# Turning the rows of the first layer's second block: VectorE squares read back from DRAM, with the scaling on Pool, against sixteen transposes on TensorE

## The chip, the cores and the metric

The kernel runs on one core of one Trainium2 chip. The metric is the device time of one execution in microseconds. Before the change it is 1894.93 us, the median of three runs (1894.68 to 1895.23).

## What is computed

Two layers, each of them an attention block and a gated block, over 2048 rows of 448 features. Both layers use the same weights.

```
x = x + A(layernorm(x), wqkv, wo)
x = x + B(layernorm(x), w_gate, w_up, w_down)
(and both once more)

A(x): q, k, v = x @ wqkv                      # 16 heads of 28
      softmax(q k^T * 28**-0.5) v, @ wo
B(x): (sigmoid(x @ w_gate) * (x @ w_up)) @ w_down
```

layernorm subtracts the mean of a row and divides by sqrt(variance + 1e-5); it has no weights. All inputs and the output are float32.

## The kernel before, in words

The 2048 rows are 16 row tiles of 128 (`NT`), and four of them (`TB`) make a block of 512 rows (`W`), so there are four blocks, b0 to b3. Matrix products are made in float16 with both operands split into a high and a low part: a product of two split operands is three matmuls, high by high, low by high and high by low.

The instructions go to each engine in the order in which the program emits them; there is no scheduler. Each engine works through its own list in order, and waits where it reads what another engine or a transfer has yet to write. SP (SyncE) and Pool (GpSimd) also issue DMAs from their lists, in order too: a DMA that has to wait keeps the ones behind it waiting.

Each layer begins with `project` (from L712 on): for each block the queries and keys and then the values are made from the block's normalized rows.

- `qk` (L725) makes queries and keys of one block in seven tiles. A tile is 11 matmuls of 128x512 (L564), accumulated in one of four banks of PSUM in turn. ScalarE evicts the high part (L756), VectorE the low part (L757), both look at squares (L759, L761) that TensorE sums later (L735, L738), and SP stores the tile to a scratch tensor in DRAM (L764). After tile i the function calls `fill[i]`, work of other kinds that is put there by hand.
- `vals` (L784) makes the values of one block, a row tile at a time: 11 matmuls of 128x448 (L586 to L591), in the same four banks, evicted by ScalarE (L793). Between the products of row tile j and its eviction it calls `after[j]`, again work put there by hand. For block 0 that list is `along_values`.

For these products a block has to be normalized and turned, so that features lie along the partitions. The kernel has two ways for it, both in class `Block`:

- Over TensorE: VectorE computes mean and variance of a row tile (L287, L288), Pool the reciprocal root of the variance (L291, L293), VectorE scales (`scale`, L320), TensorE turns 128x128 pieces into PSUM (`turn`, L508), ScalarE casts the high part from PSUM (`turned_high`, L532) and VectorE subtracts to get the low part (`turned_low`, L540 and L543). A block has 16 such transposes, four row tiles by four groups of features.
- Over DRAM: after the same norm and scaling VectorE turns each row tile in squares of 32 by 32 (`squares`, L337), SP stores the squares to DRAM in four DMAs (`store`, L349), reads them back in two with the squares put in their places (`gather`, L357 and L359), and ScalarE and VectorE split the result from SBUF (`part`, reached through `ready`: L218, L219, L223, L224). The read back waits for all four stores, and stands behind them in SP's list.

In the first layer b0 and b1 go the first way and b2 and b3 the second. In the second layer all but b0 go the second way.

The order around the change, for the first layer and block 0: the norms of b1's row tiles 0 and 1 come after tile 2 of `qk`, those of 2 and 3 after tile 3, the scaling of all four on VectorE after tile 5 (`fill` at L836). Between the value products of b0 come, after row tile 0, the allocation of b1's operands, eight transposes of b1 with their splits, and two loads for measuring the sizes of the weights (`tell.read`, L935 on, issued by SP); after row tile 1 the other eight transposes and two loads; after row tile 2 the maxima of the norms of b0 (`fin`, L775), b2's norms and a load issued by Pool; after row tile 3 b2's squares and store and another group of loads by Pool (`along_values` at L838 to L841). Then `qk` of b1 begins on TensorE.

At the very start, before any data have come, TensorE runs products of zeros (`keep_busy`, L261).

Of the kernel before, what the change touches and what calls it, by code (L numbers as in the profile page):

```python
# [19 lines left out]
P = 128  # L20
# [7 lines left out]
TB = NT // NB  # L28
W = TB * P
NF = F // P  # L30
NQ = D // 32
# [87 lines left out]
def interleaved_layers(ctx: ExitStack, tc: tile.TileContext, x_in, wqkv, wo, w_gate, w_up,  # L119
                       w_down, out):  # L120
    nc = tc.nc
# [6 lines left out]
    big = Slots(spool, "s", N_SLOTS)  # L128
# [26 lines left out]
    x = cpool.tile([P, NT, D], F32, name="x")  # L155
# [107 lines left out]
    class Block:  # L263
# [52 lines left out]
            nc.vector.transpose(self.xs[:, :, j, :], v)  # L316
            qrt.put(v)

        def scale(self, j):
            nc.vector.tensor_scalar(self.xn[:, j, :], x[:, self.b * TB + j, :],  # L320
                                    self.mv[:, j, 0:1], self.rs[:, j:j + 1],
                                    op0=ALU.subtract, op1=ALU.mult)

# [56 lines left out]
        def squared(self):  # L380
            return [lambda j=j: self.norm_two(j) for j in range(0, TB, 2)] + [
                lambda j=j: self.lift(j) for j in range(TB)] + [
                    lambda j=j: self.square(j) for j in range(TB)]
# [328 lines left out]
    def project(layer, wq, begun):  # L712
# [4 lines left out]
        def ones_of_values():  # L717
            for v in values:
                nc.gpsimd.memset(v[:, :, :, DH:VC], 0.0)
                nc.gpsimd.memset(v[:, :, :, DH:DH + 1], 1.0)  # L720
# [99 lines left out]
        idle = None  # L820
        sq = lambda b, *js: lambda: blks[b].squares(js)
        b1, b2, b3 = blks[1:]
        if layer == 0:
            def scaled():
                b1.xn = big.get("xn", [P, TB, D])
                for j in range(TB):
                    b1.scale(j)

            def turned(kts):
                b1.turn_banks(6, kts)  # L830
                for j in range(TB):
                    b1.turn(j)
                b1.turned_high()
                b1.turned_low()

            fill = [idle, idle, lambda: b1.norm([0, 1]), lambda: b1.norm([2, 3]), idle, scaled]  # L836
            tell = Measure()
            along_values = {0: lambda: (b1.parts(), turned([0, 1]), tell.read(2)),  # L838
                            1: lambda: (turned([2, 3]), big.put(b1.xn), tell.read(2)),
                            2: lambda: (fin(), b2.norm(), tell.read()),  # L840
                            3: lambda: (b2.squares(), b2.store(), tell.read())}  # L841
        else:
            ones_of_values()
            fill = [idle, lambda: b1.ready(0, 1), lambda: b1.ready(2, 3), b2.norm,
                    lambda: b2.squares([0, 1]), sq(2, 2, 3), b2.store]
            along_values = {0: b3.norm, 1: sq(3, 0, 1), 2: lambda: (fin(), b2.gather()),
                            3: sq(3, 2, 3)}
        fin = qk(0, blks[0], fill, None)
        vals(0, blks[0], along_values)
        if layer == 0:  # L850
            fill = [b2.gather, b3.norm, sq(3, 0, 1), sq(3, 2, 3), idle,
                    lambda: b2.ready(0, 1), lambda: (b2.ready(2, 3), b3.store())]
        else:
            fill = [idle, lambda: b2.ready(0, 1), lambda: b2.ready(2, 3), b3.store]
        fin = qk(1, b1, fill, None)
        vals(1, b1, {0: b3.gather, 2 if layer == 0 else 1: fin})
        add = tell.add if layer == 0 else idle
        fin = qk(2, b2, [idle, lambda: b3.ready(0, 1), lambda: b3.ready(2, 3), idle, add, add,
                         add], None)
        fin = qk(3, blks[3], [add, add, add], fin)  # L860
# [1005 lines left out]
    for layer in range(LAYERS):  # L1866
        values, heads, last_values = project(layer, wq, begun)
        gate = WeightsGated()
        outs = attend(layer, values, heads, last_values, gate, wq.keep)
        mlp_first = out_project(outs, gate)  # L1870
        wq = WeightsQKV()

        def before_next(f, wq=wq):
            if f == NF - 1:
                wq.load()

        begun = gated(layer, mlp_first, gate, before_next)
# [28 lines left out]
```

## Time and profile before

| | |
|---|---|
| median of three runs | 1894.93 us |
| span of the profiled execution, first to last instruction | 1893.0 us |
| what the median lies above the span | 1.93 us |
| busy TensorE / VectorE / ScalarE / Pool, share of the span | 100% / 76% / 73% / 12% |
| granted TensorE clock, mean | 1.000 |
| mean DMA rate | 143 GB/s |

How to read the rows that follow. A row of the order of time has the start and the duration in us, the engine, the line, the operation, what it writes and reads, the count of instructions that were merged into it, and in brackets the idle time of the engine before it with what ended it. PE is TensorE, DVE is VectorE, ACT is ScalarE, SPq is SP's list of DMA issues (the duration there is the issue, not the transfer). Matmuls are pipelined, so the duration of one is longer than the distance between two. A row of the waits has who waited for whom, and then the total in us, the number of times and the longest. A row of a group by tile has the smallest, median and largest duration in ns behind the count. A row by line has the busy time in us and the mean in ns behind the bar. A row of a table of stretches has the busy time of PE, PEld, DVE, ACT and POOL (each with its count of instructions), the granted clock, the mean share of time that the DMA engines were busy, and GB/s.

### The profile page before, as it was taken

The numbers are of one execution on the slowest core, as the hardware profiler recorded it, in microseconds if no ns is written. First come the engines' busy times: TensorE is split into PE (matmuls) and PEld (weight loads), VectorE is DVE, ScalarE is ACT, GpSimd is POOL, SyncE is SP. The second block draws the span as 40 slices with busy tenths as digits, with TensorE's granted clock in tenths as the row PEclk, the third lists the DMA queues.
The fourth block names the chain that finished last, engine by engine and source line by source line (L and its number), as shares of the span: only waits on it lengthen the run. The fifth ranks groups of instructions, "written<-read, shape, count | busy, mean of one in ns | idle before, by whom it ended". The sixth has DMA issues, their size and how long they took to land. (4 is left out here: it accounts for less than half of the span.)

```text
span 1893.0 us, 56282 instructions
## 1 busy us (share of the span) xinstructions
PE 1886.5 (100%) x24254; PEld 1323.1 (70%) x24254; DVE 1430.7 (76%) x2835; ACT 1382.7 (73%) x1772; POOL 231.5 (12%) x453
## 2 busy tenths in 40 slices
PE   9999999999999999999999999999999999999999
PEld 4455555555556799999954556667666567999998
DVE  7758989898976688787564487787778676887664
ACT  5569999999993566555345799999999745565541
POOL 3023112222101111111100000000000020121110
PEclk9999999999999999999999999999999999999999
DMA  7676454334323566646734322122120245666553
GB/s 247 194 212 166 132 137 128 107 119 129 103 88 121 192 205 235 231 181 238 251 96 134 90 52 47 32 52 52 31 48 24 67 160 174 218 251 223 208 208 142
DMA packets 110882, 270.86 MB, mean 143 GB/s; under 512 B 13214, under 2 KB 67838, under 8 KB 110496
## 3 DMA queue, kind: packets, MB, share of 16 engines
q0 software_dynamic: 31776, 158.51, 23.4%
q1 hardware_dynamic: 78288, 108.20, 20.3%
q8 instruction: 192, 3.15, 0.7%
q10 hardware_dynamic: 560, 0.46, 0.1%
q14 instruction: 66, 0.54, 0.1%
HBM read 207.88 MB, written 50.85 MB: 137 GB/s over the span
## 5 line engine op out<-in xcount | busy, mean ns | idle before, releaser
L1222 ACT ACTIVATE prob_s<-sc 128x1536 f32<-128x1536 f32 (+1 forms) x657 | 887.9, 1487 | 6.6 <-PE sc L1207 5.9
L1258 PE MATMUL acc<-prob_s,val_s 128*32 128x256 f32 (+3 forms) x7700 | 569.9, 383 | 0.0
L1207 PE MATMUL sc<-qp_s 114*32 114x512 f16 x7868 | 553.2, 379 | 0.0
L579 PEld LDWEIGHTS <-gu_s 128*128 128x128 f16 x4368 | 426.9, 98 | 46.8 <-issue 0.4
L1207 PEld LDWEIGHTS <-qp_s 114*32 114x32 f16 x8192 | 272.7, 95 | 203.4 <-issue 88.3
L1258 PEld LDWEIGHTS acc<-prob_s,val_s 128*32 128x32 f32 x7700 | 272.3, 110 | 142.9 <-issue 13.6
L579 PE MATMUL chain<-xwide_s,gu_s 128*128 128x256 f16 x2016 | 247.5, 273 | 0.0
L1552 PE MATMUL dnp<-dn_s,hparts_s 128*128 128x224 f16 x2016 | 225.2, 259 | 0.0
L1552 PEld LDWEIGHTS <-hparts_s 128*128 128x128 f16 x2016 | 194.0, 98 | 4.4
L1238 DVE SCALAR_TENSOR_TENSOR power_q<-power_q,expo_q 128x512 f32<-128x512 f32 x243 | 168.2, 692 | 8.3
L1625 ACT COPY one_q<-chain 128x256 f32<-128x256 f32 x224 | 82.4, 371 | 121.4 <-PE chain L579 120.8
L1641 DVE TENSOR_TENSOR one_q<-side,one_q 128x512 f32<-128x512 f32 x112 | 72.2, 686 | 101.8 <-PE side L579 101.5
L579 PE MATMUL side<-xshort_s,gu_s 128*128 128x256 f16 x1120 | 140.5, 273 | 0.0
L564 PE MATMUL qkp<-xhl_s,wqk_s 128*128 128x512 f16 x616 | 138.1, 379 | 0.7 <-ACT wqk_s L231 0.2
L564 PEld LDWEIGHTS <-wqk_s 128*128 128x128 f16 x616 | 60.1, 98 | 69.8 <-ACT wqk_s L231 1.1
L1437 POOL DMA_DIRECT2D gu_s<-gu_parts x104 | 56.0, 538 | 430.5 <-PE side L579 424.5
L1287 DVE STREAM_TRANSPOSE oturned_q<-acc 128x512 f32<-128x512 f32 x32 | 22.9, 716 | 97.1 <-PE acc L1258 96.9
L1258 PE MATMUL acc<-power_q,val_s 128*32 128x256 f32 (+3 forms) x300 | 94.2, 396 | 0.0
L579 PE MATMUL side<-xwide_s,gu_s 128*128 128x256 f16 x672 | 91.6, 273 | 0.0
L1505 ACT CAST hparts_s<-hsums_q 128x256 f16<-128x256 f32 (+1 forms) x136 | 65.0, 494 | 30.2 <-DVE hsums_q L1517 20.2
L756 ACT ACTIVATE qkhl_q<-qkp 128x512 f16<-128x512 f32 x56 | 33.2, 593 | 71.9 <-PE qkp L564 68.3
L1652 ACT ACTIVATE one_q<-one_q 128x512 f32<-128x512 f32 x56 | 35.2, 629 | 64.3 <-DVE one_q L1641 64.3
(218 smaller groups left out, 2318.0 us busy)
## 6 DMA issues: line engine op xcount, KB each, us to landing
gu_s<-gu_parts POOLq DMA_DIRECT2D x104, 800.0 KB, 6.0
dn_s<-dn_parts POOLq DMA_DIRECT2D x42, 784.0 KB, 7.8
qp_s<-qk_scr SPq DMA_DIRECT2D x96, 224.0 KB
qk_scr<-qkhl_q SPq DMA_DIRECT2D x56, 256.0 KB
gu_parts<-pack_s POOLq DMA_DIRECT2D x14, 800.0 KB, 3.8
xt_scr<-xs_s SPq DMA_DIRECT2D x48, 224.0 KB
xraw_s<-xt_scr SPq DMA_DIRECT2D x12, 768.0 KB
qp_s<-qk_scr SPq DMA_DIRECT2D x64, 112.0 KB
```

Source lines behind the costliest of these rows:

```text
L564: nc.tensor.matmul(pm, w, x, start=(i == 0), stop=(i == len(terms) - 1))
L579: nc.tensor.matmul(pm, a, x, start=(first and i == 0), stop=(i == len(terms) - 1), skip_group_check=True)
L1207: nc.tensor.matmul(ps[32 * j:32 * j + 32, :], hd.k[:, keys], hd.q[:, qb * W:(qb + 1) * W], start=True, stop=True, tile_position=(0, 32 * j))
L1222: nc.scalar.activation(prob[:, 0:n, :], ps[:, 0:n, :], AF.Exp, scale=exp_scale)
L1238: nc.vector.scalar_tensor_tensor(p, p, c[k], y, op0=ALU.add, op1=ALU.mult)
L1258: nc.tensor.matmul(acc[qb * VC:(qb + 1) * VC, s], v[:, kc % TB, h, :], probs[c * NB + qb][:, s], start=(kc == 0 and a == 0), stop=(kc == N ...
L1437: queue.dma_start(self.gu[-1][m], gu_parts[p, m])
L1505: nc.scalar.copy(to[:, :, 0], a)
L1552: nc.tensor.matmul(pm, a[:, x, t], w[:, p, y], start=(begin and n == 0 and (j == 0 or alone)), stop=(n == 2), skip_group_check=True)
L1625: nc.scalar.copy(to, pm)
L1641: nc.vector.tensor_tensor(one[m], side[m], one[m], op=ALU.add)
L1652: nc.scalar.activation(out, v, AF.Sigmoid, scale=gate_scale)
```

## The change

Block b1 of the first layer goes the second way instead of the first. Its scaling moves from VectorE to Pool. The norms move one `qk` tile forward (after tiles 1 and 2), the scaling follows after tile 3, the squares after tiles 4 and 5, and store and read back after tile 5, ahead of the store of tile 6 in SP's list. The splits come between the value products of b0, after row tiles 2 and 3. What stood there moves: b2's norms come after row tile 0, two of its squares after row tile 1, the other two with `fin` and b2's store after row tile 3. The second layer is as before.

```
-        def scale(self, j):
-            nc.vector.tensor_scalar(self.xn[:, j, :], x[:, self.b * TB + j, :],
+        def scale(self, j, engine=nc.vector):
+            engine.tensor_scalar(self.xn[:, j, :], x[:, self.b * TB + j, :],
                                     self.mv[:, j, 0:1], self.rs[:, j:j + 1],
                                     op0=ALU.subtract, op1=ALU.mult)
...
             def scaled():
                 b1.xn = big.get("xn", [P, TB, D])
+                b1.xs = big.get("xs", [P, NQ, TB, 32])
                 for j in range(TB):
-                    b1.scale(j)
-
-            def turned(kts):
-                b1.turn_banks(6, kts)
-                for j in range(TB):
-                    b1.turn(j)
-                b1.turned_high()
-                b1.turned_low()
-
-            fill = [idle, idle, lambda: b1.norm([0, 1]), lambda: b1.norm([2, 3]), idle, scaled]
+                    b1.scale(j, nc.gpsimd)
+
+            def squared(*js):
+                for j in js:
+                    nc.vector.transpose(b1.xs[:, :, j, :], b1.xn[:, j, :])
+                if js[-1] == TB - 1:
+                    big.put(b1.xn)
+                    b1.store()
+                    b1.gather()
+
+            fill = [idle, lambda: b1.norm([0, 1]), lambda: b1.norm([2, 3]), scaled,
+                    lambda: squared(0, 1), lambda: squared(2, 3)]
             tell = Measure()
-            along_values = {0: lambda: (b1.parts(), turned([0, 1]), tell.read(2)),
-                            1: lambda: (turned([2, 3]), big.put(b1.xn), tell.read(2)),
-                            2: lambda: (fin(), b2.norm(), tell.read()),
-                            3: lambda: (b2.squares(), b2.store(), tell.read())}
+            along_values = {0: lambda: (b2.norm(), tell.read(2)),
+                            1: lambda: (sq(2, 0, 1)(), tell.read(2)),
+                            2: lambda: (b1.ready(0, 1), tell.read()),
+                            3: lambda: (b1.ready(2, 3), fin(), sq(2, 2, 3)(), b2.store(),
+                                        tell.read())}
```

## The prediction

> **What bounds the kernel now.** I read the page first, then the list of waits of TensorE, then the order of time around the change.
>
> ```profile
> span 1893.0 us, 56282 instructions
> ...
> PE 1886.5 (100%) x24254; PEld 1323.1 (70%) x24254; DVE 1430.7 (76%) x2835; ACT 1382.7 (73%) x1772; POOL 231.5 (12%) x453
> ...
> PE 44%; DVE 0%; issue 0%
> ```
>
> ```profile
> PE still L261 <- DVE warm L179: 1.3, 1, 1.3
> PE turn L508 <- DVE xn_s L320: 0.8, 1, 0.8
> PE qkp L564 <- ACT wqk_s L231: 0.2, 1, 0.2
> PE qkp L564 <- DVE xhl_s L543: 0.2, 1, 0.2
> ```
>
> The second fence is the whole list for the whole span: TensorE waits four times, 2.5 us in all. So TensorE sets the end, and every microsecond taken from its queue or put into it moves the end by as much, since nothing behind it has idle time to give. The question is what its queue looks like between 30 and 50 us, where the first layer goes from block 0 to block 1:
>
> ```profile
> 33.48 1.66 PE L508 MATMUL turn<-ident,xn_s 128*128 128x128 f32 x8
> 34.98 0.35 PE L589 MATMUL vp<-wv_s,xhl_s 128*128 128x448 f16 x1
> ...
> 37.07 1.04 PE L508 MATMUL turn<-ident,xn_s 128*128 128x128 f32 x8
> 37.94 0.35 PE L589 MATMUL vp<-wv_s,xhl_s 128*128 128x448 f16 x1
> ...
> 42.43 9.66 PE L564 MATMUL qkp<-xhl_s,wqk_s 128*128 128x512 f16 x44
> 51.92 0.27 PE L735 MATMUL qnorm<-sq_q,ind 128*128 128x256 bf16 x1
> ```
>
> The two groups of eight transposes stand between value products of block 0; at 42.43 block 1's products begin, 44 of them in 9.49 us, so 0.216 each and 2.37 for a tile of 11.
>
> **What it removes.** The first group holds the queue from 33.48 to 34.98 (part of it waiting for the last scaled rows), the second from 37.07 to 37.94: 1.50 + 0.87 = 2.37 us. Without them TensorE asks for block 1's operands at 42.43 - 2.37 = 40.06. The four evictions of the transposes on ScalarE and VectorE give way to four casts and four subtractions from SBUF of the same kind, and cost nothing new.
>
> **What it adds: a chain that has to end at 40.06.** It is norms, Pool's scaling, VectorE's squares, store, read back, split. VectorE's queue is in order, so I place the squares in it:
>
> ```profile
> 22.25 1.82 DVE L234 SCALAR_TENSOR_TENSOR wqk_s<-wraw_s,up,wqk_s 128x1536 f16<-128x1536 f32 x1 [1.17 <-ACT wqk_s L231]
> ...
> 24.79 0.62 DVE L287 BATCH_NORM_STATS2 st<-x 128x6 f32<-128x448 f32 x1
> ...
> 26.27 0.66 DVE L757 SCALAR_TENSOR_TENSOR qkhl_q<-qkp,qkhl_q 128x512 f16<-128x512 f32 x1
> 27.04 0.62 DVE L287 BATCH_NORM_STATS2 st<-x 128x6 f32<-128x448 f32 x1
> ...
> 28.42 0.18 DVE L288 BATCH_NORM_AGGREGATE mv<-st 128x2 f32<-128x6 f32 x1
> ...
> 32.87 1.78 DVE L320 TENSOR_SCALAR xn_s<-x,mv,rs 128x448 f32<-128x448 f32 x4
> ```
>
> ```profile
> L337 DVE STREAM_TRANSPOSE xs_s<-xn_s x16: 645/645/648, 45.9 to 984.1; 128x448 f32<-128x448 f32 x16
> ```
>
> A pair of norms takes 26.27 - 24.79 = 1.48. The first pair moves one tile up, in front of the subtraction at 22.25, where VectorE is idle for 1.17: that subtraction starts 0.31 later. TensorE's tile 4 reads its result, so TensorE may lose up to 0.3 there; the long wait that follows covers it. The second pair moves into the first one's place. Two squares come in ahead of tile 5's eviction: 2 x 0.645 = 1.29. So VectorE is through with tile 5 not at 32.87 but at 32.87 - 1.48 + 0.31 + 1.29 = 33.0. Two more squares end at 34.3, if Pool is in time.
>
> ```profile
> 28.97 0.70 POOL L293 TENSOR_TENSOR rs<-rs,nhalf 128x2 f32<-128x2 f32 x1
> ```
>
> ```profile
> L433 POOL MEMSET xraw_s<- 64x512 f32 x6 | 3.2, 528 | 0.2
> ...
> L200 POOL CAST ind<-ind_f_q 128x128 bf16<-128x128 f32 x1 | 0.3, 289 | 0.0
> ```
>
> Now the second pair ends at 28.60 and Pool's reciprocal root at 29.67; the pair now runs 1.48 - 0.31 sooner and also passes tile 3's eviction (27.04 - 26.27 = 0.77), 1.94 in all, so 27.7. No row shows Pool scaling 448 elements. From below a memset gives 0.528/512 x 448 = 0.46 us, from above a cast 0.289/128 x 448 = 1.01. I take 0.75, the middle. Then the four row tiles are scaled at 28.5, 29.2, 30.0 and 30.7. VectorE would come to the first two squares near 28.4 and 29.1 and to the fourth near 33.6, so Pool is just in time; at 1.01 the second square comes 0.6 later, at 0.46 nothing changes. The store starts at **34.3** (34.2 to 34.9).
>
> Store and read back (four DMAs out, two in, 896 KB each way) stand in the trace for other blocks, from the first store to the cast that waited for the data:
>
> ```profile
> 65.58 3.43 SPq L349 DMA_DIRECT2D xt_scr<-xs_s  x4
> ```
>
> ```profile
> 79.20 1.14 ACT L218 CAST xhl_s<-xraw_s 128x512 f16<-128x512 f32 x2 [4.75 <-DMA xraw_s<-xt_scr]
> ```
>
> ```profile
> 975.74 3.42 SPq L349 DMA_DIRECT2D xt_scr<-xs_s  x4
> ```
>
> ```profile
> 987.76 1.14 ACT L218 CAST xhl_s<-xraw_s 128x512 f16<-128x512 f32 x2 [2.21 <-DMA xraw_s<-xt_scr]
> ...
> 988.41 1.29 DVE L219 TENSOR_TENSOR xhl_s<-xraw_s,xhl_s 128x512 f16<-128x512 f32 x2 [2.08 <-ACT xhl_s L218]
> ```
>
> That is 13.6 and 12.0. The second had a queue as empty as this one will be. But the loads that Pool issues for the weights' sizes follow block 2's norms, which now come earlier, and fall on the read back; so I take 12.8, the middle. The data are there at 34.3 + 12.8 = **47.1**, seven microseconds after they are asked for.
>
> The split follows in turn. ScalarE's two casts end at +0.60 and +1.14, VectorE's subtractions at +1.34 and +1.94. ScalarE's queue then holds the eviction of a value tile before the other two casts:
>
> ```profile
> 40.22 0.54 ACT L793 ACTIVATE val_s<-vp 128x448 f32<-128x448 f32 x1 [0.69 <-PE vp L587]
> ```
>
> ```profile
> L223 ACT CAST xhl_s<-xraw_s x6: 612/613/617, 65.2 to 1014.1; 64x512 f16<-64x512 f32 x6
> L224 DVE TENSOR_TENSOR xhl_s<-xraw_s,xhl_s x6: 684/686/686, 66.0 to 1015.0; 64x512 f16<-64x512 f32 x6
> ```
>
> So the third cast ends near +2.2, the third subtraction at +2.9, the last at +3.65. TensorE's first tile can use each part as it comes; its last two products run after +3.65, and it ends at +4.1 at full speed.
>
> **The clock of TensorE after the wait.** The trace has matmuls of this width in two paces:
>
> ```profile
> 1.25 4.87 PE L261 MATMUL still<-still_q 128*128 128x512 f16 x11 [1.25 <-DVE warm L179]
> ```
>
> ```profile
> 28.81 2.54 PE L564 MATMUL qkp<-xhl_s,wqk_s 128*128 128x512 f16 x11
> ```
>
> Eleven take 4.87 after TensorE had been idle, 2.54 when it had not, though the page's granted clock is full in both. Elsewhere TensorE is never idle for more than the 0.8 of the list; seven microseconds are more like the time before the start, so I expect the slow pace again. At 0.44 a product, with the same arrivals, the tile ends at +5.75, not +4.1, so the cost is 1.65, the rest of the 2.33 lying under the arrivals. The Trainium skill ("TensorE: Matmul & The Clock Gate", Part 1) says that the array falls to half its clock after an idle window of about 3.4 us and needs about as long a busy one to leave it; by that rule the stall is long enough, and the start's rows agree with its factor of two.
>
> **Sum.** In before the first tile of block 1 ends at 42.43 + 2.37 = 44.80; now at 47.1 + 5.75 = 52.85: **+8.05 us**. The saving of 2.37 is in it already (it only makes the wait longer). What else waits: ScalarE stands at its cast, with two value evictions behind it, which hold no bank that block 1's first tile needs. VectorE stands at its subtraction, with block 2's last squares and store behind it. These run 3 us after +3.65, the store at 53.8, its data 13.6 later at 67.4, split by 71.5.
>
> ```profile
> 68.24 9.66 PE L564 MATMUL qkp<-xhl_s,wqk_s 128*128 128x512 f16 x44
> ```
>
> Block 2 is wanted at 68.24 + 8.05 = 76.3, so this is hidden, with some 5 us to spare. On SP tile 6's store and the weight reads fall behind the read back; they are for sums and heads tens of microseconds on. Layer two is unchanged. The span becomes 1901.05; the median of before, 1894.93, lies 1.93 above its span, and with the same surround I forecast **1903.0 us**.
>
> **Rivals.**
> 1. The wait is there but TensorE keeps its pace: +8.05 - 1.65 = +6.4, 1901.3. For it: the granted clock never falls in this trace. Against: the first eleven products.
> 2. Pool or the transfers are worse: Pool at 2 us a tile ends the fourth scaling at 35.7 and with the last square the store starts near 36.4, 2.1 late: 1905.1. A trip of 13.6 on top of that is 1905.9. Against: no Pool row of plain arithmetic is near 4.5 ns an element.
> 3. The other side, **faster**: the read back comes in time. It decides at a round trip of 40.06 - 0.65 - 34.3 = 5.1 us; below it TensorE only loses the transposes: 1894.93 - 2.37 = 1892.6. The best rate in sight is this window's last number, in GB/s:
>
> ```profile
> 42.00:44.00 2.00, 2.00 (x12) 0.93 (x10) 1.79 (x6) 0.54 (x1) 0.02 (x1) 1.00 1.04 383
> ```
>
>    0.918 MB at 383 GB/s is 2.4 us, 4.8 for both ways with no latency at all. Both measured trips are over twice that.
> 4. In between, **no difference**: each way takes its bytes at that rate and the time to be reported done.
>
> ```profile
> 72.00:74.00 2.00, 2.00 (x11) 0.90 (x10) 0.58 (x3) 0.85 (x3) 0.00 (x0) 1.00 0.04 7
> ```
>
> ```profile
> 73.73 0.38 SPq L357 DMA_DIRECT2D xraw_s<-xt_scr  x1
> ```
>
>    The transfers are over by 72 (7 GB/s are left), and the read back, which waits for the store, is issued 1.7 later. So 2 x (2.4 + 1.7) = 8.2, and the change is 34.3 + 8.2 + 4.1 - 44.80 = +1.8, 1896.7, if that shorter wait leaves the pace alone. The Trainium skill ("DMA: Bandwidth & Descriptors", Anatomy of one DMA) has a fit, 2.0 us and the bytes at 436 GB/s, though for Pool's path, by which the trip would be 8.2 too. Against it stand the whole trips of 12.0 and 13.6.
>
> **Chances.** Forecast 0.62; rival 1, 0.20; rival 2, 0.09; rival 3, 0.04; rival 4, 0.05. A difference under 0.2% (3.8 us) I call none; it is about what a measurement of this kernel can tell. Slower then has 0.62 + 0.20 + 0.09 = 0.91, same 0.05, faster 0.04. The range runs from rival 1 with a trip of 11.2, as far under the shortest measured as the middle is above it (1903.0 - 1.65 - 1.6 = 1899.7), over the forecast with a trip of 13.6 and a store at 34.9 (1904.4), to the middle of rival 2's two times (1905.5): **1899.7 to 1905.5**.
>
> **What would show it.** In the changed profile TensorE's list of waits should have a new first row, block 1's product (L564) waiting for a cast or subtraction of the split, 5 to 8 us; the store should start near 34.3, the cast near 47, and the first eleven products after it should take about 5 us. No wait at block 2 should appear. I am wrong if the trip is under 9 us, if the squares wait for Pool by more than 1 us, or if TensorE makes time up elsewhere.

## The result, and the profile after

The changed kernel takes **1908.15 us** (median of five runs, 1905.07 to 1909.66) against 1895.23 for the kernel before (five runs, 1894.68 to 1895.87): ratio 1.0066, 95% interval 1.0056 to 1.0077. It is slower, as forecast, but by 13 us and not by 8: the time lies 2.65 us above the upper end of the forecast's range. The profiled execution of the changed kernel is its shortest run, 1905.07, with a span of 1903.2, 10.2 above the span of before.

The page's head and TensorE's whole list of waits, changed kernel:

```profile
span 1903.2 us, 56260 instructions
...
PE 1886.9 (99%) x24238; PEld 1345.1 (71%) x24238; DVE 1431.8 (75%) x2835; ACT 1383.2 (73%) x1772; POOL 241.2 (13%) x457
```

```profile
PE qkp L564 <- ACT xhl_s L218: 9.2, 1, 9.2
PE still L261 <- DVE warm L179: 1.3, 1, 1.3
PE vp L590 <- DVE wv_s L234: 1.2, 1, 1.2
PE qkp L564 <- DVE wqk_s L234: 0.3, 1, 0.3
PE turn L508 <- DVE xn_s L320: 0.3, 1, 0.3
PE qkp L564 <- ACT wqk_s L231: 0.2, 1, 0.2
PE qkp L564 <- DVE xhl_s L543: 0.2, 1, 0.2
```

The sixteen transposes are gone from TensorE (16 instructions fewer), and a new first row stands in the list: block 1's product waits 9.2 us for the split. Two smaller waits are new as well, 1.2 for the low part of the values' weights and 0.3 at tile 4; both stand ahead of the long one, which covers them. The order of time shows the chain on Pool, VectorE, SP, ScalarE and TensorE:

```profile
27.19 8.26 POOL L320 TENSOR_SCALAR xn_s<-x,mv,rs 128x448 f32<-128x448 f32 x4
```

```profile
29.12 0.65 DVE L832 STREAM_TRANSPOSE xs_s<-xn_s 128x448 f32<-128x448 f32 x1 [1.07 <-POOL xn_s L320]
30.98 0.65 DVE L832 STREAM_TRANSPOSE xs_s<-xn_s 128x448 f32<-128x448 f32 x1 [1.21 <-POOL xn_s L320]
...
35.48 0.65 DVE L832 STREAM_TRANSPOSE xs_s<-xn_s 128x448 f32<-128x448 f32 x1 [0.41 <-POOL xn_s L320]
```

```profile
36.16 3.03 SPq L349 DMA_DIRECT2D xt_scr<-xs_s  x4
42.35 0.38 SPq L357 DMA_DIRECT2D xraw_s<-xt_scr  x1
```

```profile
49.86 1.14 ACT L218 CAST xhl_s<-xraw_s 128x512 f16<-128x512 f32 x2 [12.44 <-DMA xraw_s<-xt_scr]
...
55.24 0.60 ACT L756 ACTIVATE qkhl_q<-qkp 128x512 f16<-128x512 f32 x1 [2.33 <-PE qkp L564]
```

```profile
50.53 11.79 PE L564 MATMUL qkp<-xhl_s,wqk_s 128*128 128x512 f16 x44 [9.20 <-ACT xhl_s L218]
```

Read it from the end. The first eviction of block 1 starts at 55.24, 5.4 us after the first cast at 49.86. That cast waited for the read back, issued at 42.35 (a leg of 7.5 us), which waited for the store begun at 36.16 (a leg of 6.2): a trip of 13.7. The store waited for the squares, and three of the four squares for Pool, 2.7 us in all.

The stretches of two microseconds around the wait (the granted clock, the share of the DMA engines and GB/s are the last three columns):

```profile
42.00:44.00 2.00, 0.00 (x0) 0.00 (x0) 1.68 (x3) 0.00 (x0) 2.00 (x5) 1.00 0.62 185
44.00:46.00 2.00, 0.00 (x0) 0.00 (x0) 0.00 (x0) 0.00 (x0) 1.73 (x3) 0.58 1.01 327
46.00:48.00 2.00, 0.00 (x0) 0.00 (x0) 0.00 (x0) 0.00 (x0) 0.00 (x0) 0.50 0.98 300
...
54.00:56.00 2.00, 2.00 (x9) 0.84 (x8) 1.93 (x5) 0.73 (x2) 0.00 (x0) 0.85 1.05 336
...
64.00:66.00 2.00, 2.00 (x11) 0.98 (x10) 1.93 (x5) 1.12 (x2) 0.00 (x0) 1.00 0.42 139
```

The granted clock falls to 0.50 while TensorE waits and is back at 1.00 during the stretch from 54. And the DMA engines are full while nothing else runs: Pool is issuing its seven loads (41.2 to 45.7) beside the read back. They come free at about 64.8. In the trace of before that is at about 56.5:

```profile
54.00:56.00 2.00, 2.00 (x11) 0.96 (x10) 1.32 (x5) 1.23 (x2) 1.22 (x2) 1.00 1.08 314
56.00:58.00 2.00, 2.00 (x11) 0.98 (x10) 1.93 (x4) 0.88 (x2) 0.00 (x0) 1.00 0.24 78
```

### The profile page after: what moved, and what is told of

It reads as the page before. It is cut to its first block, busy times and chain, and to the rows that moved or that the text cites. A ratio compares the mean times of both kernels' runs of the same rounds, so it can differ in the third digit from the quotient of the medians.

```text
span 1903.2 us, 56260 instructions
## 1 busy us (share of the span) xinstructions
PE 1886.9 (99%) x24238; PEld 1345.1 (71%) x24238; DVE 1431.8 (75%) x2835; ACT 1383.2 (73%) x1772; POOL 241.2 (13%) x457
## 5 line engine op out<-in xcount | busy, mean ns | idle before, releaser
L1262 PE MATMUL acc<-prob_s,val_s 128*32 128x256 f32 (+3 forms) x7700 | 576.2, 384 | 0.0
L1211 PE MATMUL sc<-qp_s 114*32 114x512 f16 x7868 | 558.9, 379 | 0.0
L1211 PEld LDWEIGHTS <-qp_s 114*32 114x32 f16 x8192 | 284.7, 95 | 193.0 <-issue 79.0
L1262 PEld LDWEIGHTS acc<-prob_s,val_s 128*32 128x32 f32 x7700 | 285.7, 110 | 131.7 <-issue 12.4
L564 PE MATMUL qkp<-xhl_s,wqk_s 128*128 128x512 f16 x616 | 140.1, 382 | 10.2 <-ACT xhl_s L218 9.2
```

The source lines that it names most:

```text
L564: nc.tensor.matmul(pm, w, x, start=(i == 0), stop=(i == len(terms) - 1))
L1211: nc.tensor.matmul(ps[32 * j:32 * j + 32, :], hd.k[:, keys], hd.q[:, qb * W:(qb + 1) * W], start=True, stop=True, tile_position=(0, 32 * j))
L1262: nc.tensor.matmul(acc[qb * VC:(qb + 1) * VC, s], v[:, kc % TB, h, :], probs[c * NB + qb][:, s], start=(kc == 0 and a == 0), stop=(kc == N ...
```

## The experiments

My theory after the result: the loss is the long wait and the cold clock behind it, and the wait is longer than forecast because Pool scales slowly and because Pool's loads for the weights' sizes share the DMA engines with the read back. Rivals: VectorE's own queue sets the store whoever scales, the transfers are slow by themselves, and some other part of the change costs as well. Each ratio below is against runs of the kernel before on the same chip (medians 1895.05 to 1895.40).

### e1_keep_warm: products in the place of the wait

```
         vals(0, blks[0], along_values)
+        if layer == 0:
+            pm = bank(6, "still")
+            for i in range(34):
+                nc.tensor.matmul(pm, wq.qk[0][:, 0, 0:P], wq.qk[0][:, 1, 0:W], start=(i == 0),
+                                 stop=(i == 33))
```

> The changed kernel with 34 products of weights by weights, into a bank that nobody reads, put in TensorE's queue between block 0's values and block 1's queries (34 x 0.216 = 7.3 us, in a wait of 9.2). Clock theory: the wait let the granted clock fall to half, and the first tile after it ended 5.2 us after the data where 4.1 is possible, so this kernel is 1 to 2 us faster than the changed one, its mean clock is 1.000 and its runs lie closer together. Rival, the wait alone: the clock costs nothing because the first tile waits for its operands in any case: same time, within 0.3 us. If the spread of the changed kernel's runs (1905.1 to 1909.7) stays, it is the transfers' and not the clock's.

Measured: 1909.12 (1906.70 to 1910.00), ratio 1.0070 [1.0056, 1.0084]. Inconclusive on the clock: the products end at 48.4, but the data came only at 53.4 in this run, TensorE still waited 5.7 and cooled (the granted clock fell at 52). What it did show is the read leg: issue at 42.10, first cast at 53.39, 11.3 us where the changed kernel's profile has 7.5.

```profile
42.10 0.38 SPq L357 DMA_DIRECT2D xraw_s<-xt_scr  x1
```

```profile
53.39 1.14 ACT L218 CAST xhl_s<-xraw_s 128x512 f16<-128x512 f32 x2 [16.25 <-DMA xraw_s<-xt_scr]
```

### e2_scale_vector: VectorE scales, the rest as changed

```
-                    b1.scale(j, nc.gpsimd)
+                    b1.scale(j)
```

> The changed kernel with the scaling of block 1 left on VectorE (four times 0.5 us in place of four times 2.1 on Pool), all else as changed. Theory that Pool delays the store: the store starts at 35.0 to 35.2 in place of 36.2, the value products of block 0 no longer wait 1.2 us for the split of the weights, and the time falls by about 1.1 us. Rival, VectorE's own queue sets the store: the scaling's 2 us there take the place of the waits for Pool, and the time stays within 0.4 us.

Measured: 1908.19 (1904.16 to 1909.52), ratio 1.0061 [1.0047, 1.0075]: no difference from the changed kernel. No square waits for Pool now, and the store starts at 35.60, in a run whose values began 0.85 later (first product 32.04 against 31.19), so 1.4 earlier by the run's own start. But the read leg of this profile is 11.5 (41.80 to 53.32), which buries it. Pool's scaling delays the store by some 1.4 us against VectorE's. What that is worth in the time is not shown: no run scales on VectorE while Pool's loads are out of the way.

### e3_loads_later: Pool's loads moved behind the read back

```
-                            2: lambda: (b1.ready(0, 1), tell.read()),
-                            3: lambda: (b1.ready(2, 3), fin(), sq(2, 2, 3)(), b2.store(),
-                                        tell.read())}
+                            2: lambda: b1.ready(0, 1),
+                            3: lambda: (b1.ready(2, 3), fin(), sq(2, 2, 3)(), b2.store())}
...
-            fill = [b2.gather, b3.norm, sq(3, 0, 1), sq(3, 2, 3), idle,
+            fill = [b2.gather, b3.norm, sq(3, 0, 1), sq(3, 2, 3), lambda: tell.read(2),
```

> The changed kernel with the seven loads that Pool issues (1.47 MB, at 41.2 to 45.7 in the changed profile) moved to block 1's queries, so that nothing else of Pool's runs beside block 1's read back. Theory that the loads stretch the read back: from its issue to the cast it takes 5.2 to 5.5 us in place of 7.5, and the time falls by about 2 us. Rival: the read back is stretched by what SP has queued behind it or not at all by the loads: within 0.4 us.

Measured: 1904.84 (1904.22 to 1906.82), ratio 1.0053 [1.0039, 1.0066], 3.3 below the changed kernel. The read leg is 5.4:

```profile
42.60 0.38 SPq L357 DMA_DIRECT2D xraw_s<-xt_scr  x1
```

```profile
48.01 1.14 ACT L218 CAST xhl_s<-xraw_s 128x512 f16<-128x512 f32 x2 [10.34 <-DMA xraw_s<-xt_scr]
```

### e5_pool_scale: the kernel before, with early norms and Pool's scaling

```
-                    b1.scale(j)
+                    b1.scale(j, nc.gpsimd)
...
-            fill = [idle, idle, lambda: b1.norm([0, 1]), lambda: b1.norm([2, 3]), idle, scaled]
+            fill = [idle, lambda: b1.norm([0, 1]), lambda: b1.norm([2, 3]), scaled]
```

> The kernel before with two parts of the change alone: norms one tile earlier and scaling on Pool, while TensorE still does the sixteen transposes. Theory: at 2.1 us a row tile Pool ends near 35.4 instead of VectorE near 34.5, so the first transposes wait about 1 us longer and the kernel is 0.5 to 1.2 us slower than before; most of the change's loss is then not Pool's. Rival, Pool hinders VectorE on a wider front: 3 us or more.

Measured: 1896.54 (1895.81 to 1899.34) against 1895.05, ratio 1.0007 [0.9998, 1.0016]. With the transposes kept, the median is 1.5 us higher, and the interval still holds no change. Its trace has the last two of the first eight transposes waiting 1.4 for the fourth row tile. So Pool's scaling by itself does not make most of the 13 us.

### e4_early_norms: the kernel before, with early norms, VectorE scaling

The same edit of `fill` as above, `b1.scale(j)` unchanged.

> The kernel before with block 1's norms one tile earlier and its scaling after tile 3, all on VectorE; the transposes stay on TensorE. Theory: the scaled rows are there before the first group of transposes, which waits for them now (0.8 us in the list of waits); up to 0.3 is lost at tile 4, whose weights' split starts later. So 0.3 to 0.6 faster, 1894.5 where before is 1895.05. Rival: the wait moves to the split of the values' weights, which then comes later on VectorE (1.2 us in the changed kernel): 0.2 to 0.7 slower.

Measured: 1894.60 (1894.11 to 1896.63) against 1895.40, ratio 0.9997 [0.9988, 1.0006]. The median is 0.8 lower, the interval holds no change. In the trace the transposes' own wait is gone (the first group takes 1.04 where it took 1.66) and 0.33 is lost at tile 4, as expected. It is the lowest median of all kernels run, by less than this measurement can tell.

### e6_later_and_warm: e3 with 33 products in the place of the wait

The edits of e3 and of e1 together, with 33 products.

> The kernel with Pool's loads later (1904.84 us, where TensorE waited 7.1 us and the first tile of block 1 then ended 6.3 us after its data), with 33 products that nobody reads behind block 0's values: 7.1 us of work in the place of the wait. Theory (the idle array's clock costs some 1.7 to 2 us): the granted clock stays at 1.00, the first tile ends 4.1 to 4.5 us after its data, and the time is near 1903.0, 1.5 to 2.2 below the kernel without the products. Rival (the split's arrivals hold the first tile up, not the clock): the tile still ends some 6 us after its data and the time is within 0.4 of 1904.8. If the products outlast the wait, the time is above 1904.8.

Measured: 1905.20 (1903.17 to 1906.58), ratio 1.0053 [1.0037, 1.0068]. The mechanism is as the theory has it and the time as the rival has it. ScalarE's rows give the first: first cast and first eviction of block 1 are 4.2 apart, where e3 has 5.9 (48.01 and 53.87).

```profile
47.92 1.14 ACT L218 CAST xhl_s<-xraw_s 128x512 f16<-128x512 f32 x2 [10.25 <-DMA xraw_s<-xt_scr]
...
52.12 0.60 ACT L756 ACTIVATE qkhl_q<-qkp 128x512 f16<-128x512 f32 x1 [1.17 <-PE qkp L564]
```

The list of waits gives the second. TensorE, now earlier, waits where it had not waited before, behind block 2's split:

```profile
PE knorm L738 <- DVE sq_q L761: 1.5, 1, 1.5
```

Two more rows are new in that list, but they stand elsewhere: 0.4 at block 1's own second product (49.31), which waits for its subtraction, and 0.5 at 125 us, behind the branch of L909. In the profiles block 1 gains 2.4 over e3 and block 2's products begin only 0.7 earlier (77.04 against 77.74).

VectorE's list has block 2's subtractions (L219) ahead of the last tile's low part and squares (L757, L761), and TensorE's look at those norms (L738) comes ahead of the values' last row tile. So block 2's trip is wanted at L738, and not only at block 2's products 2.2 us later.

### e7_loads_on_sp: Pool's loads on SP's list, behind the read back

```
-                queue = nc.sync if kind == "o" or j < 3 and kind == "d" else nc.gpsimd
+                queue = nc.sync
```

> The changed kernel with all the loads for the weights' sizes on SP's list, in their old places in the program: those that Pool issued beside the read back now stand behind it in SP's list. Theory (what stretches the read back is transfers of another list that share the DMA engines with it while it runs): from the issue of the read back to the first cast 5.4 us as with later loads, and a time near 1904.8. Rival (the bytes themselves hold it up, whichever list issues them, or the read leg is that long anyway): 7 us and more from issue to cast, 1907 to 1909.

Measured: 1905.25 (1904.81 to 1906.40), ratio 1.0054 [1.0038, 1.0069]. Read leg 5.1:

```profile
42.52 0.39 SPq L357 DMA_DIRECT2D xraw_s<-xt_scr  x1
```

```profile
47.63 1.14 ACT L218 CAST xhl_s<-xraw_s 128x512 f16<-128x512 f32 x2 [10.06 <-DMA xraw_s<-xt_scr]
```

Behind it in the same list, the same bytes cost block 1's read back nothing. In the changed kernel, from 42.3 to 50, Pool's queue moved 1.26 MB in 52.8% of the engines' time and SP's 1.00 MB in 41.6%: SP's queue, with the read back in it, got less than half of them.

```profile
q0 software_dynamic: 355, 1.26, 52.8%
q1 hardware_dynamic: 561, 1.00, 41.6%
```

### e8_early_data: block 1 without its trip

Block 1's operands in the first layer are read from rows of the weight matrix at the start; the squares and their store stay, their read back goes. The kernel leaves out block 1's dependence on its own normalized rows.

```
-                    b1.gather()
...
+            def early():
+                b1.raw = big.get("xraw", [P, 4, W])
+                nc.sync.dma_start(b1.raw[:, 0:3, :],
+                                  wqkv[0:384, 0:W].rearrange("(k p) n -> p k n", p=P))
+                nc.sync.dma_start(b1.raw[0:64, 3, :], wqkv[384:448, 0:W])
...
-            fill = [idle, lambda: b1.norm([0, 1]), lambda: b1.norm([2, 3]), scaled,
+            fill = [early, lambda: b1.norm([0, 1]), lambda: b1.norm([2, 3]), scaled,
```

> The changed kernel, where block 1's operands in the first layer are read at the start of queries and keys from rows of the weight matrix of the same size, and not from block 1's turned rows (the store of the squares stays, their read back goes); so it leaves out the dependence of block 1 on the trip. Theory (the loss is the wait for the trip and the cold clock after it, nothing else): no wait at block 1, the transposes' 2.37 us saved, 1.2 lost where the values wait for the split of their weights and up to 0.3 at tile 4, so 1893.8 to 1894.6. Rival (something else in the change costs as well, on VectorE, SP or the DMA engines): above 1896.

Measured: 1903.53 (1903.12 to 1904.80), ratio 1.0045 [1.0029, 1.0060]. **My theory fell here.** Without any trip to wait for, 8 of the 13 us are still lost:

```profile
PE qkp L564 <- DVE xhl_s L219: 2.8, 1, 2.8
PE knorm L738 <- DVE sq_q L761: 2.3, 1, 2.3
```

The first wait is VectorE's order: the subtractions stand behind block 2's norms, scaling and two squares, where the change put them because block 1's data would be late. The second is block 2's trip again, 20.0 us (49.78 to 69.74).

The two are only 5.1 of the loss. The granted clock fell to 0.50 at each of them, and the products behind took longer than in before: 43 of block 1 in 11.13 us, where 44 take 9.66, and the last eleven of the values 3.69 (72.70 to 76.39), where they take 2.08. That is 1.7 and 1.6.

```profile
44.94 11.13 PE L564 MATMUL qkp<-xhl_s,wqk_s 128*128 128x512 f16 x43 [2.80 <-DVE xhl_s L219]
```

With the expected 1.2 and 0.3, and 0.8 more of waiting at the first transposes of the kernel, less the 2.37, it is 8.3, which is what the span rose by (1901.3 against 1893.0).

### e9_early_data_order: e8 with the old order of the splits

```
-            along_values = {0: lambda: (b2.norm(), tell.read(2)),
-                            1: lambda: (sq(2, 0, 1)(), tell.read(2)),
-                            2: lambda: (b1.ready(0, 1), tell.read()),
-                            3: lambda: (b1.ready(2, 3), fin(), sq(2, 2, 3)(), b2.store(),
-                                        tell.read())}
+            along_values = {0: lambda: (b1.ready(0, 1), tell.read(2)),
+                            1: lambda: (b1.ready(2, 3), tell.read(2)),
+                            2: lambda: (fin(), b2.norm(), tell.read()),
+                            3: lambda: (b2.squares(), b2.store(), tell.read())}
```

> The kernel with block 1's operands read early from the weight matrix (1903.53 us; it leaves out block 1's dependence on its own normalized rows), with the splits of block 1 back after block 0's value tiles 0 and 1, ahead of block 2's norms and squares, as the kernel before has them. Theory (with the data early the loss came from VectorE's order, made for late data, which held up the split at block 1 and then block 2's store): no wait of over 0.5 us at block 1 nor at block 2's split, the transposes' 2.37 us saved, 1.2 lost at the values' weights and 0.3 at tile 4, so 1894 to 1895. Rival (early loads and Pool's scaling disturb something else): the waits stay and the time is above 1898.

Measured: 1903.83 (1902.44 to 1907.65), ratio 1.0042 [1.0028, 1.0056]. Half of the expectation failed. There is no wait at block 1 at all, and a larger one behind block 2's split (this profile is of the longest run, whose first tiles also come 4 us late, so its instants are not to be set beside the others'):

```profile
PE knorm L738 <- DVE sq_q L761: 7.3, 1, 7.3
```

```profile
53.74 9.96 SPq L349 DMA_DIRECT2D xt_scr<-xs_s  x4
...
69.12 0.38 SPq L357 DMA_DIRECT2D xraw_s<-xt_scr  x1
```

```profile
74.54 1.14 ACT L218 CAST xhl_s<-xraw_s 128x512 f16<-128x512 f32 x2 [12.92 <-DMA xraw_s<-xt_scr]
```

Block 2's trip takes 20.8 us, 53.74 to 74.54, of which 15.4 are the store's leg. In before the same trip began at 49.91 and ended at 62.45, 12.5. What is new ahead of it are block 1's store and what that pushed back.

### e10_warm_b2_first: e6 with block 2's squares and store ahead of block 1's split

```
                             0: lambda: (b2.norm(), tell.read(2)),
-                            1: lambda: (sq(2, 0, 1)(), tell.read(2)),
+                            1: lambda: (b2.squares(), b2.store(), tell.read(2)),
                             2: lambda: b1.ready(0, 1),
-                            3: lambda: (b1.ready(2, 3), fin(), sq(2, 2, 3)(), b2.store())}
+                            3: lambda: (b1.ready(2, 3), fin())}
```

> The kernel with later loads and 33 products in the place of the wait (1905.2 us), with all of block 2's scaling and squares, and its store, ahead of block 1's split on VectorE and SP. Theory (the 2 us that the warm clock won came back as waits behind block 2's split, whose store had stood behind block 1's split): block 2's store starts near 46 in place of 54.4, TensorE's waits at the last look at the norms (1.5 us), at the values behind it (0.5) and at block 2's products (0.4) go, and the time is 1902.5 to 1903.5. Rival (the store of block 2 now runs beside the read back of block 1 and stretches it by as much): the first cast after 49, and 1904.5 or more.

Measured: 1903.42 (1903.27 to 1904.74), ratio 1.0043 [1.0029, 1.0057]. The time is as expected, the waits only in part: the store starts at 46.52, the wait at the norms falls from 1.5 to 0.8 and does not go, the 0.5 goes, and the 0.4, which I had put at block 2's products, stands at block 1's second product and stays (0.3). Block 1's read back is not stretched (47.64 - 42.19 = 5.45). The granted clock is 1.000 for the whole span. This is the lowest median of the kernels that turn block 1 over DRAM, 4.7 below the change and still 8.3 above before.

```profile
46.52 6.07 SPq L349 DMA_DIRECT2D xt_scr<-xs_s  x4
```

Block 2's read back is stretched instead. It is issued at 59.09, Pool's moved loads from 60.08 on, and its leg is 11.3, where the changed kernel has 5.5 for block 2 (66.15 to 71.66):

```profile
70.41 1.14 ACT L218 CAST xhl_s<-xraw_s 128x512 f16<-128x512 f32 x2 [5.21 <-DMA xraw_s<-xt_scr]
```

So moving the loads has moved the collision, at least in part. How much of the remaining 8.3 us that is, no run here tells.

### e11_after_again: the changed kernel once more

> The changed kernel once more, on the same chip as the two others and as a second sample of its spread: if Pool's loads beside the read back cost some 3 us, its median is again 1907 to 1909 with runs from 1905 to 1910, and a profiled run of 1908 or so shows a read leg (issue of the read back to the first cast) of 10 us or more. If its first median was a feature of that chip, it is near 1905, the time of the kernels with the loads moved.

Measured: 1907.27 (1906.99 to 1908.00), ratio 1.0062 [1.0045, 1.0078]. The size of the loss came again. Its profiled run, 1906.99, has a read leg of 8.4, not the 10 or more that I had expected near 1908:

```profile
42.58 0.38 SPq L357 DMA_DIRECT2D xraw_s<-xt_scr  x1
```

```profile
50.99 1.14 ACT L218 CAST xhl_s<-xraw_s 128x512 f16<-128x512 f32 x2 [13.36 <-DMA xraw_s<-xt_scr]
```

### e12_early_data_loads_later: e9 with Pool's loads later still

Like e8 and e9 it leaves out block 1's dependence on its own rows.

```
-                            2: lambda: (fin(), b2.norm(), tell.read()),
-                            3: lambda: (b2.squares(), b2.store(), tell.read())}
+                            2: lambda: (fin(), b2.norm()),
+                            3: lambda: (b2.squares(), b2.store())}
...
-        vals(1, b1, {0: b3.gather, 2 if layer == 0 else 1: fin})
+        vals(1, b1, {0: (lambda: (b3.gather(), tell.read(2))) if layer == 0 else b3.gather,
+                     2 if layer == 0 else 1: fin})
```

> The kernel with block 1's operands read early from the weight matrix and the old order of the splits (1903.83 us, where TensorE waited 7.3 us behind block 2's split; it leaves out block 1's dependence on its own normalized rows), with Pool's loads for the weights' sizes moved behind block 2's read back, after block 1's value tile 0. Theory (the DMA engines are full from 38 to 56 us even before the change, so what it adds there comes back at block 2): block 2's trip falls to 15 us or less from the 20.8 it took, the wait of 7.3 us goes, and the time is 1894 to 1896. Rival (block 2's trip stays long because of the store of block 1 and the stores of the tiles alone): a wait of 2 us or more behind block 2's split and 1898 or more.

Measured: 1900.16 (1898.10 to 1901.40), ratio 1.0025 [1.0014, 1.0035]. 3.7 better than e9, so Pool's loads were part of what held block 2 up, but a wait of 4.5 stays and the rival's numbers hold. Block 2's trip is 16.1 (49.73 to 65.85), and then ScalarE waits for a tile's store to land before it can square the last tile:

```profile
69.52 0.63 ACT L759 ACTIVATE sq_q<-qkhl_q 128x512 bf16<-128x512 f16 x1 [2.04 <-DMA qk_scr<-qkhl_q]
```

```profile
PE knorm L738 <- DVE sq_q L761: 4.5, 1, 4.5
```

The new place of the loads may be partly to blame. Pool issued them from 60.88 on and block 2's read back had been issued at 60.32, so they ran beside each other after all, and beside the tiles' stores that stand behind the read back in SP's list. The read leg is no longer for it, 5.5; the store's leg is 10.6 of the 16.1. What of the 4.5 is block 1's store and what the moved loads, no run here tells apart.

## Why the prediction was wrong in size

**What bounds the kernel, the sign, and the place of the wait: right.** TensorE's wait for the split is the new first row, and the time lost shows one for one in the span.

**"I take 0.75, the middle" for Pool's scaling: the first failed step.** It also exceeded the bound of 1.01 that I had set from a cast.

```profile
L320 POOL TENSOR_SCALAR xn_s<-x,mv,rs x4: 1871/1884/2692, 27.2 to 32.8; 128x448 f32<-128x448 f32 x4
```

A row tile takes 1.88 (4.2 ns an element), the last 2.69, four 8.26. "Pool is just in time" was false: the squares waited 2.7 us and the store started at 36.16 instead of 34.3. Rival 2, to which I gave 0.09, had this price and this instant almost to the point (2 us a tile, 36.4). A memset and a cast are no neighbours of an operation that takes a mean and a scale for each row; VectorE's own four had cost 1.78, and nothing in the trace said that Pool could do one in 0.75. This share of the loss is read from instants; e2, which takes it away, is not measurably faster.

**"I take 12.8, the middle" for the trip: the second failed step.** The prediction named Pool's loads as falling on the read back, and then priced that as the middle between two trips that had not met this. (A third one in before, block 2's, began on full engines at 49.91 and took 12.5 all the same, but the engines were free again by 56.5, ahead of its read back at 57.07.) Without the loads beside it the read leg is 5.1 to 5.5 (e3, e6, e7, e10), so that the whole trip is 11.3 to 11.7 with the store's leg of 6.2. With them it is 7.5, 8.4, 11.3 and 11.5 (the changed kernel twice, e1, e2), and the times of these runs rise with it: 1905.07, 1906.99, 1909.12 and 1909.52. The row from which I took "the best rate in sight" had a DMA share of 1.04 one column before it. A full resource stood in my own fence, and I read only its GB/s. Rival 4's 8.2 us failed from the other side: even without the loads the trip takes 11.3 or more, and the store moves at 182 GB/s (38 to 40) and not at 383. The fit of the Trainium skill ("DMA: Bandwidth & Descriptors", Anatomy of one DMA), from which 8.2 is an estimate too, falls short by as much.

**The clock: right.** I forecast a first tile that ends 5.75 after the data at the slow pace and 4.1 at full speed. From first cast to first eviction it took 5.4 in the changed kernel, 5.9 in its second run (50.99 to 56.85) and in e3 and e7, and 4.2 with the clock held up (e6, e10). The Trainium skill ("TensorE: Matmul & The Clock Gate", Part 1) puts both the idle time before the fall and the busy time before the return at about 3.4 us. In the changed kernel TensorE went idle at 41.33 (50.53 - 9.20), the clock fell 3.0 us later and was back 4.1 us after the products resumed (both instants from the mean clock of their stretches), one a little under and one a little over that figure. What the cold clock costs in the time is less sure: e6 kept it up and its median is no lower than e3's, because of the wait that came instead.

**The sum, mended.** For the profiled run: +8.05, and 1.9 for the store, 0.9 for the trip, less 0.4 for the tile, is +10.4; the span rose by 10.2. (The 0.2 between them is in the start of the sum: it took the first tile of before to end at 44.80, and its eviction starts at 45.00; from there to 55.24 is 10.24.) The three errors add up to 2.4, so the profiled run, 1905.07, still lies inside the forecast's range. The median lies 3.1 above that run, and by what follows it is the read leg that carries it out of the range. The kernels with the loads moved are 2.9 and 3.3 below the median, and the second profiled run shows how: read leg 0.9 longer, first eviction 1.6 later, span 2.0 longer. What makes the leg 7.5 and 8.4 in the changed kernel and 11.3 and 11.5 in e1 and e2, with the same transfers, stays open.

**"This is hidden, with some 5 us to spare" for block 2: wrong, though it cost nothing in the changed kernel.** I measured the spare at block 2's products. But the first to be held up is TensorE's last look at the norms, through VectorE's list. In the changed kernel VectorE's squares for it end at 74.40 and the third of the looks comes at 76.29 (76.07 + 0.49, less 0.27 for one of them):

```profile
74.12 0.28 DVE L761 TENSOR_TENSOR sq_q<-sq_q 128x256 bf16<-128x256 bf16 x1
```

```profile
76.07 0.49 PE L738 MATMUL knorm<-sq_q,ind 128*128 128x256 bf16 x3
```

The spare was 1.9. In e6 to e10 and e12, where block 1 came sooner, it was gone: TensorE waits there for 0.4 (e7) to 7.3 us (e9).

**Rival 3, "if the read back comes in time ... 1892.6": its price was wrong.** Block 1's data were there in time in e8, e9 and e12, and the times were 1903.5, 1903.8 and 1900.2. In none of them did an early arrival bring the 2.37 us of the transposes. Block 2's trip grew from 12.5 to between 16.1 and 20.8, and in before it had 0.9 us to spare at the same look (squares through at 65.20, third look at 66.06). The likely reason is the added store: in e8 the DMA engines are full until about 64, in before until about 56.5. These three kernels have 0.9 MB of early reads of their own and Pool's scaling, so the exact split is not theirs to give. What they show is that the changed kernel's long wait hid a second cost.

## What to carry to other kernels

Before a transfer is added, read the DMA share of the stretch where it will run: where it is near 1, price the trip by the bytes already queued there, and put loads that nobody needs yet behind it. When something is declared hidden, look for the first instruction of the bounding engine that stands behind it in any in-order list, and not for the one that uses the data. An operation that the trace does not show on an engine is priced from the nearest operation with the same operands, and the rival that says "several times slower" gets more than a tenth.

## What the runs showed of the hardware

- Pool's subtract-and-scale of 128x448 float32 took 1.87 to 1.88 us, over four times VectorE's 0.445 (1.78 for four). The fourth took 2.69. It began at 32.76, while VectorE ran its two-input L234 (31.55 to 33.64), and its extra 0.8 is about what L234 still ran, 0.9. In e5 it was the second that began under L234, and that one took 3.00 (32.07, with L234 running to 33.4). A row tile that had begun before L234 kept its time in both (30.91 to 32.76, 30.18 to 32.07), and so did L234 (2.17 here, 2.22 in before). The Trainium skill ("SBUF — State Buffer", Who interferes with whom) says that a VectorE instruction with two inputs in SBUF and a Pool instruction that reads SBUF lock each other out of a shared port. The lengthened row tiles fit that, the overlap at full pace before them does not; no run here separates the cause.
- The store of 0.9 MB in 512-byte pieces keeps the DMA engines full at less than half of the rate of the weight loads: in the changed kernel 0.97 of the engines at 182 GB/s, against 1.06 at 385 in before. From the first store to the issue of the read back it took 6.2 us in all eight profiles where block 1 is read back.

```profile
38.00:40.00 2.00, 2.00 (x12) 1.07 (x11) 1.73 (x6) 0.00 (x0) 0.08 (x1) 1.00 0.97 182
```

```profile
48.00:50.00 2.00, 2.00 (x11) 0.90 (x10) 1.93 (x5) 0.88 (x2) 1.82 (x3) 1.00 1.06 385
```

- The clock can fall sooner than after 3 us: in e8 an idle time of 2.34 us, from 70.2 to 72.54, was enough, and the products behind it ran at half pace for over 3 us. Behind the same kernel's wait of 2.80, from 42.14 to 44.94, it fell at about 45.2, when the products had already begun again (the stretch from 45 has a mean of 0.61). A wait of 1.51 in e6 left it at 1.00.

```profile
72.00:73.00 1.00, 0.46 (x2) 0.25 (x2) 0.91 (x3) 1.00 (x4) 0.00 (x0) 0.76 0.47 164
73.00:74.00 1.00, 1.00 (x4) 0.44 (x3) 0.95 (x2) 1.00 (x4) 0.00 (x0) 0.50 0.49 157
```
